# GpSimd writes the padding of q and k, two more PSUM banks, and a new order of steps in a fused attention and soft mixture-of-experts kernel

## The chip, the cores and the metric

The kernel runs on one core of one Trainium2 chip. The core has five engines that each work through a queue of their own: TensorE (PE, matrix products), VectorE (DVE), ScalarE (ACT), GpSimd (POOL) and SyncE (SP, which here only issues DMA transfers). Transfers go between the chip's memory and the on-chip buffers by sixteen DMA engines. The metric is the time of one execution on the device in microseconds (us), as the median of several runs. All times inside an execution are counted from the start of its span, the time from its first to its last instruction.

## The reference

Two stages, cut to what is computed:

```python
# attention over columns: B, N, C = 4, 5056, 256
qn = q / (norm(q, axis=1) + 1e-6)          # each column over all N rows
kn = k / (norm(k, axis=1) + 1e-6)
a = softmax(kn.T @ qn / tau)               # C x C for each batch
x = (v @ a).reshape(B * N, C)
# soft mixture of experts: 8 experts with 4 slots each, F = 1024
logits = x @ phi                           # (B*N) x 32
d = softmax(logits, axis=0)                # over all rows
slots = (d.T @ x).reshape(8, 4, C)
slot_out[e] = relu(slots[e] @ w1[e]) @ w2[e]
out = softmax(logits, axis=1) @ slot_out   # 20224 x 256
```

Every output row depends on the experts' output, and that on the softmax over all rows, so all of q, k and v must be read before the first output can be stored.

## The kernel before

Each batch is cut into ten units of 512 rows (UB = 10, UT = 512), so 5120 rows of which 5056 are real. The host pads q and k with zeros: in a batch's last unit (`u % 10 == 9`) the fourth of its four tiles of 128 rows has 64 real rows (HD = 64), and zeros in the other half. `load_qk` (L113) fetches a unit's q and k side by side in one transfer of 1 MB into one of five `raw` buffers (NRAW = 5). ACT casts and squares the unit (`cast` L177, `square` L208), DVE makes the low halves of a split into two reduced-precision parts and adds up the squares (`low` L183, `add` L214), PE adds k^T q into S (`score` L234). After ten units the batch's `att_` steps make the matrix a; GpSimd takes the root of the norms (L256).

v comes in both layouts, `v` (L126) and transposed `vt` (L132, L134); a part of the transposed tiles is turned on chip instead (`vTp` L359, `x` L364). PE makes the logits (L386), ACT copies them into `lg` (L405), DVE takes their running maximum (L415), ACT the exponentials (L449), DVE turns them into weights (L464), and PE gathers the slot sums (G, L486). A short run of `finish_`, `join_` and `last_` steps ends with the slots' inputs, `slT` (L604).

Then the experts. `up` (L672) makes H for the experts 0 to 3 (r = 0) and 4 to 7 (r = 1), each in two halves x of 512 columns: H0_0, H0_1, H1_0, H1_1. `relu` (L682) writes them to hs, `flip_h` (L688) turns hs into hTp, `back_h` (L694) copies that to hT, on DVE for x = 0 and on ACT for x = 1. `down` (L703) multiplies with w2 into O0 and O1, the two halves of the 256 output columns; each is 64 rows of the order, 128 instructions on PE. `o_copy` (L715) copies O to `ob` on DVE, `o_fold` (L719) spreads it on PE, and `o_back` (L725) writes `so` on ACT.

Beside this each batch has its softmax over the slots, on a tile `nat` of 128 x 1280: the transpose of the logits (L421), maximum, subtraction, exponential, sum, 1e-9 and reciprocal, product (`cm`, `cs`; L610 to L628), and the transpose back into `lg` (`c_flip`, L634). `out_mul` (L743) multiplies these with `so`, `out_evict` copies the result from PSUM into a tile `o` (ACT L765 for even g, DVE L767 for odd g), and `store` writes it. Batch 0's five tiles go in two half stores each of 512 KB, one for each half hf of the columns (L775), so that they may start when O0 is there and O1 is not; all others are stored whole, 1 MB each (L773).

PSUM has eight banks: S0, S1, T0, T1, LB, GB, X0, X1. O0 lies in T0 and O1 in T1. `out_mul` takes four banks for each product, in turn from the list `rings[hf]`, from place 4k on, where k counts the products.

All steps are entered in a list `plan` by `at(...)` and `tail(...)`. The table ORDER, 985 numbers, then says in which order they are called, and thus the order in each engine's queue. The first number given to `tail` has no part in it. All transfers are issued from SP's queue, in that order, and one that waits holds those behind it.

The lines that set the banks, the order and the two halves of the output:

```python
rings = {0: [S0, S1, LB, GB, T0, X0], 1: [S0, S1, LB, GB, T0, X0, T1, X1]}
t = bank(ring[(4 * k + g) % len(ring)], f"op{b}_{p}_{hf}_{g}")
for x in ORDER:
    key, _, f, a = plan[x]
    f(*a)
```

Of the kernel before, what the change touches and what calls it, by code (L numbers as in the profile page):

```python
# [17 lines left out]
UB = 10  # L18
# [11 lines left out]


ORDER = [
# [43 lines left out]
]  # L76


@with_exitstack
def colnorm_attention_soft_moe(  # L80
    ctx: ExitStack,
    tc: tile.TileContext,
    qk: bass.AP,
    v8: bass.AP,
    vt8: bass.AP,
    vt7: bass.AP,
# [26 lines left out]
    def load_qk(u, parts=((0, 4),)):  # L113
        b, i = divmod(u, UB)
        raw = apool.tile([P, 4, 2, C], F32, tag="raw", name=f"raw{u}", bufs=NRAW)
        for lo, hi in parts:
            src = qk[b, i][:, : 8 * C].rearrange("p (j x c) -> p j x c", x=2, c=C)
            sp.dma_start(raw[:, lo:hi], src[:, lo:hi])
        raws[u] = raw

    vs, vts = {}, {}
# [604 lines left out]


    OT = ["raw"] * 3 + ["hl"] * 3 + ["v"] * 6 + ["raw"] * 5 + ["hl"] * 3
    rings = {0: [S0, S1, LB, GB, T0, X0], 1: [S0, S1, LB, GB, T0, X0, T1, X1]}
    rings[None] = rings[1]  # L730
    ots, ops = {}, {}

# [277 lines left out]
        tail(28.07 + x, back_h, 1, x)  # L1010
        for r in range(2):
            for f in range(0, NF, 2):
                tail(30 + 5 * x + 2 * r + 0.1 * f, down, r, x, f)
        tail(34.6 + 5 * x, o_copy, x)
        tail(34.7 + 5 * x, o_fold, x)
        tail(34.8 + 5 * x, o_back, x)
# [76 lines left out]
```

## Time and profile before

| | |
|---|---|
| median of 3 runs | 284.16 us (283.67 to 284.9) |
| profiled execution | 283.62 us |
| its span | 281.8 us |
| mean granted TensorE clock | 0.951 |
| busy: PE, DVE, ACT, POOL | 251.1, 236.2, 189.8, 18.0 us |
| DMA | 114.55 MB in all, mean 406 GB/s |

How to read it: busy times are sums over an engine's instructions within the span. The profiled execution is one run more, with the profiler on; its span leaves out 1.8 us that lie around the first and last instruction. The share of the DMA is the mean over sixteen engines of the time that their packets took, which overlap a little, so that a full stretch reads 1.01 or 1.02.

### The profile page before, as it was taken

To read this page: it belongs to the slowest core of one execution; us is meant where nothing else is said; L and a number is where in the kernel's file an instruction comes from. 1 tells how busy PE (TensorE), PEld (TensorE's weight loads), DVE (VectorE), ACT (ScalarE), POOL (GpSimd) and SP (SyncE) were. 2 spreads that over 40 slices of the span, in tenths; PEclk is the share of its full clock that TensorE was granted. 3 is DMA by queue.
4 is the path that set the end of the run, shared out by engine and by line. 5 is a ranking of instruction groups with operands and counts; after the bars stand their busy time and mean duration, and the time that the engine had idled before them with its cause. 6 is when DMAs were issued, how large, how long until landed. Compare 5 with 4: busy or idle time off the path is not lost.

```text
span 281.8 us, 6011 instructions
## 1 busy us (share of the span) xinstructions
PE 251.1 (89%) x2446; PEld 204.7 (73%) x2446; DVE 236.2 (84%) x347; ACT 189.8 (67%) x273; POOL 18.0 (6%) x10
## 2 busy tenths in 40 slices
PE   8898999999999999999999999998989899659700
PEld 7687999999989989788686778755544778337500
DVE  1599999999999899999979695479988899998800
ACT  4879788889998978799687945647416237544600
POOL 0000000270003500020000001000000000000000
PEclk9999999999999999999999999999999999865955
DMA  7999999999999999999999999999999999999996
GB/s 279 428 414 417 422 422 413 421 416 420 419 417 421 416 420 417 420 420 409 408 411 419 414 419 412 417 416 416 419 412 408 406 363 359 417 419 417 416 420 259
DMA packets 19612, 114.55 MB, mean 406 GB/s; under 512 B 2305, under 2 KB 2305, under 8 KB 8961
## 3 DMA queue, kind: packets, MB, share of 16 engines
q1 hardware_dynamic: 19584, 114.17, 98.8%
q8 instruction: 19, 0.31, 0.4%
q14 instruction: 9, 0.07, 0.1%
HBM read 93.19 MB, written 20.97 MB: 405 GB/s over the span
## 4 chain that ended last, share of the span: by engine, by line
DVE 40%; PE 24%; issue 11%; ACT 9%; DMA 8%; POOL 2%; DVEq 0%; SPq 0%; ACTq 0%; POOLq 0%
DVE sq L214 15%; DVE hl L183 8%; DMA raw<-in_qk_dram 6%; PE S L234 5%; PE op_None L743 5%; ACT sq L208 3%; PE H L672 3%; PE O L703 3%; PE op L743 2%; POOL rn L256 2%; DMA vt<-in_vt_dram 2%; ACT hl L177 2%; DVE mxs L415 2%; DVE o L767 2%; ACT o L765 2%
## 5 line engine op out<-in xcount | busy, mean ns | idle before, releaser
L214 DVE TENSOR_TENSOR sq<-sq,sq 128x1024 f32<-128x1024 f32 (+1 forms) x63 | 84.6, 1371 | 3.0 <-ACT sq L208 2.6
L208 ACT ACTIVATE sq<-raw 128x2048 f32<-128x2048 f32 x40 | 75.9, 1909 | 12.0 <-DVE sq L214 8.1
L234 PE MATMUL S<-raw 128*128 128x256 f32 x312 | 75.1, 381 | 2.5 <-DMA raw<-in_qk_dram 2.5
L234 PE MATMUL S<-hl 128*128 128x256 f32 x468 | 68.4, 295 | 0.0
L234 PEld LDWEIGHTS S<-raw 128*128 128x128 f32 x312 | 56.1, 190 | 9.8 <-DMA raw<-in_qk_dram 3.8
L234 PEld LDWEIGHTS S<-hl 128*128 128x128 f32 x468 | 60.4, 190 | 3.0 <-issue 1.6
L183 DVE TENSOR_TENSOR hl<-raw,hl 128x1024 fp32r<-128x1024 f32 x39 | 46.8, 1217 | 7.9 <-ACT hl L177 7.9
L177 ACT CAST hl<-raw 128x1024 fp32r<-128x1024 f32 x39 | 40.1, 1040 | 7.0 <-PE S L234 4.1
L743 PE MATMUL op_None<-so,lg 32*128 32x256 f32 x240 | 24.2, 483 | 6.3 <-ACT o L765 2.4
L256 POOL TENSOR_TENSOR rn<-rn,half 128x4 f32<-128x4 f32 x4 | 17.3, 4313 | 154.4 <-DVE rn L251 154.4
L743 PEld LDWEIGHTS op_None<-so,lg 32*128 32x128 f32 x240 | 17.7, 230 | 12.0 <-ACT o L765 7.4
L765 ACT COPY o<-op_None 128x512 f32<-128x512 f32 x30 | 16.0, 591 | 11.6 <-PE op_None L743 10.1
L767 DVE COPY o<-op_None 128x512 f32<-128x512 f32 x30 | 18.8, 680 | 2.2 <-PE op_None L743 2.2
L486 PE MATMUL G<-v,dn 128*32 128x256 f32 x320 | 19.3, 381 | 0.0
L359 PE MATMUL vTp<-ident,v 128*128 128x128 f32 x112 | 16.9, 277 | 1.0 <-ACT x L364 0.8
L364 ACT COPY vt<-vTp 128x512 f32<-128x512 f32 x22 | 12.8, 581 | 7.2 <-PE vTp L359 7.2
L386 PE MATMUL L<-vt,M 128*32 128x256 f32 (+1 forms) x272 | 17.2, 380 | 0.1
L359 PEld LDWEIGHTS vTp<-ident,v 128*128 128x128 f32 x112 | 12.9, 141 | 4.6 <-issue 1.6
L486 PEld LDWEIGHTS G<-v,dn 128*32 128x32 f32 x320 | 10.0, 110 | 6.5 <-issue 0.7
L386 PEld LDWEIGHTS L<-vt,M 128*32 128x32 f32 x272 | 8.3, 109 | 6.6 <-issue 1.3
L405 ACT COPY lg<-L 128x256 f32<-128x256 f32 x20 | 7.0, 371 | 6.7 <-PE L L386 5.5
L765 ACT COPY o<-op 128x256 f32<-128x256 f32 x20 | 6.4, 379 | 7.0 <-PE op L743 7.0
(115 smaller groups left out, 248.8 us busy)
## 6 DMA issues: line engine op xcount, KB each, us to landing
raw<-in_qk_dram SPq DMA_DIRECT2D x40, 1024.0 KB, 9.2
v<-in_v_dram SPq DMA_DIRECT2D x20, 1024.0 KB, 10.8
out_dram<-o SPq DMA_DIRECT2D x15, 1024.0 KB, 8.7
vt<-in_vt_dram SPq DMA_DIRECT2D x19, 512.0 KB, 9.1
w<-in_moe_w_dram SPq DMA_DIRECT2D x16, 512.0 KB, 11.3
w<-in_moe_w_dram SPq DMA_DIRECT2D x8, 1024.0 KB, 15.6
out_dram<-o SPq DMA_DIRECT2D x10, 512.0 KB, 4.4
vt<-in_vt_dram SPq DMA_DIRECT2D x4, 480.0 KB, 11.4
```

Source lines behind the costliest of these rows:

```text
L177: act.copy(hl[:, :ns, 0::2, :], raws[u][:, :ns])
L183: dve.tensor_tensor(hl[:, :ns, 1::2, :], raws[u][:, :ns], hl[:, :ns, 0::2, :].bitcast(F32), op=ALU.subtract)
L208: act.activation(sq, raws[u], AF.Square)
L214: dve.tensor_tensor(a[:, lo:hi], a[:, lo:hi], s[:, lo:hi], op=ALU.add)
L234: pe.matmul(sm, w, x, start=first, stop=False, skip_group_check=True)
L256: pool.tensor_tensor(rn, rn, half, op=ALU.pow)
L359: pe.transpose(tp[:, P * jj : P * jj + P], vs[p][:, 4 * h + jj, P * m : P * m + P], ident)
L386: pe.matmul(L[S * g : S * g + S, :n, :], M[:, m, :], x[:, :n, S * g : S * g + S], start=m == 0, stop=m == 1,)
L486: pe.matmul(gp[S * g : S * g + S, :C], dn[:, x, j, :], vt[:, j, :], start=x == 0 and j < G, stop=x == n - 1 and j >= G,)
L743: pe.matmul(ops[b, p, hf, g][:, h, :], cT[b][S * g : S * g + S, 4 * i : 4 * i + 4, :].rearrange("s j t -> s (j t)"), so[S * g : S * g + S] ...
L765: act.copy(dst, src)
L767: dve.tensor_copy(dst, src)
```

## The change

Three edits. `load_qk` no longer fetches the zeros of each batch's last unit: GpSimd fills rows 64 to 127 of the fourth tile, one transfer (128 x 1536 elements, 768 KB) brings the first three tiles, and another (64 x 512, 128 KB) the real half of the fourth. The bank list of the first half's products has twenty places, the four of each product k = 0 to 4 in turn: product 2 takes T1 and X1 besides T0 and X0, of which T1 is O1's, so O1 must wait until that product is copied out. The third edit is a new table ORDER. All line numbers from L119 on move by 4 or 5 in the changed kernel.

```diff
@@ ORDER
-    626, 1, 0, 7, 2, 4, 3, 13, 23, 5, 8, 12, 11, 14, 22, 41, 32, 9, 10, 18, 19, 756, 16, 17, 34, 35, 20, 21, 25, 26,
+    626, 1, 0, 7, 2, 4, 13, 5, 14, 8, 9, 10, 22, 3, 11, 12, 18, 19, 32, 23, 590, 587, 16, 17, 21, 31, 25, 26, 29, 30,
...
@@ load_qk
         raw = apool.tile([P, 4, 2, C], F32, tag="raw", name=f"raw{u}", bufs=NRAW)
+        src = qk[b, i][:, : 8 * C].rearrange("p (j x c) -> p j x c", x=2, c=C)
+        if i == UB - 1:
+            parts = ((0, 3),)
+            pool.memset(raw[HD:, 3], 0.0)
         for lo, hi in parts:
-            src = qk[b, i][:, : 8 * C].rearrange("p (j x c) -> p j x c", x=2, c=C)
             sp.dma_start(raw[:, lo:hi], src[:, lo:hi])
+        if i == UB - 1:
+            sp.dma_start(raw[:HD, 3], src[:HD, 3])
...
-    rings = {0: [S0, S1, LB, GB, T0, X0], 1: [S0, S1, LB, GB, T0, X0, T1, X1]}
+    rings = {0: [S0, S1, LB, GB, T0, X0, S0, S1, T0, X0, T1, X1, LB, GB, T0, X0, S0, S1, LB, GB], 1: [S0, S1, LB, GB, T0, X0, T1, X1]}
...
-                tail(30 + 5 * x + 2 * r + 0.1 * f, down, r, x, f)
+                tail(30 + 6 * x + 2 * r + 0.1 * f, down, r, x, f)
```

What the table moves is read from each engine's queue. On PE, first, at the end of the products H. The rows before, the last four of H1_1 and what follows (names are tile, experts, half; w1_4 is expert 4's first matrix):

```order
L672 MATMUL H1_1_2237<-w1_4_2152,slT_116 32x512
L672 MATMUL H1_1_2237<-w1_5_2222,slT_116 32x512
L672 MATMUL H1_1_2237<-w1_6_2220,slT_116 32x512
L672 MATMUL H1_1_2237<-w1_7_2224,slT_116 32x512
L688 MATMUL hTp0_0_2250<-ident_88,hs0_2189 128x128 x4
L688 MATMUL hTp0_1_2269<-ident_88,hs0_2189 128x128 x4
L688 MATMUL hTp1_0_2281<-ident_88,hs1_2226 128x128 x4
L688 MATMUL hTp1_1_2293<-ident_88,hs1_2226 128x128 x4
L703 MATMUL O0_2305<-w2_0_2259,hT0_2255 32x128
```

And after the change, from the last row of H1_0 on:

```order
L676 MATMUL H1_0_2236<-w1_7_2224,slT_116 32x512
L692 MATMUL hTp0_1_2245<-ident_88,hs0_2199 128x128 x4
L692 MATMUL hTp0_0_2251<-ident_88,hs0_2199 128x128 x4
L676 MATMUL H1_1_2258<-w1_4_2129,slT_116 32x512
L676 MATMUL H1_1_2258<-w1_5_2220,slT_116 32x512
L676 MATMUL H1_1_2258<-w1_6_2233,slT_116 32x512
L676 MATMUL H1_1_2258<-w1_7_2224,slT_116 32x512
```

The turning of the first experts' h now stands ahead of H1_1, which follows in eight rows. Behind these come 16 of O0's 64 rows, then hTp1_0 and hTp1_1, and then O0's other 48 rows.

ACT's queue in the same place, before (hs is the relu, nat the exponential of one batch's softmax, its number the batch):

```order
L682 ACTIVATE hs0_2189<-H0_0_2208,rz_114 128x512
L616 ACTIVATE nat2_2204<-nat2_2204 128x1280
L682 ACTIVATE hs1_2226<-H1_0_2227,rz_114 128x512
L682 ACTIVATE hs1_2226<-H1_1_2237,rz_114 128x512
L694 COPY hT0_2255<-hTp0_1_2269 128x512
L616 ACTIVATE nat3_2087<-nat3_2087 128x1280
L694 COPY hT1_2286<-hTp1_1_2293 128x512
```

And after:

```order
L686 ACTIVATE hs1_2235<-H1_0_2236,rz_114 128x512
L698 COPY hT0_2256<-hTp0_1_2245 128x512
L620 ACTIVATE nat2_2222<-nat2_2222 128x1280
L686 ACTIVATE hs1_2235<-H1_1_2258,rz_114 128x512
L698 COPY hT1_2310<-hTp1_1_2305 128x512
L620 ACTIVATE nat3_2226<-nat3_2226 128x1280
```

The copy hT0 has moved ahead of both exponentials, batch 2's exponential stands behind the relu of H1_0 and ahead of that of H1_1, and batch 3's behind the copy hT1. On DVE, in the same stretch, the transpose (L421) of batch 3's logits has moved from ahead of slT to behind it, next to that of batch 2; the order there is two transposes, two maxima, the subtraction of batch 2, hT0, the subtraction of batch 3, the sum of batch 2, hT1, reciprocal and product of batch 2, ob; and three small steps for rz (L586 to L588) now stand ahead of slT.

DVE's queue from the copy ob of the first half on, before (o_4 is batch 0's fifth tile, op its product with first or second half of the columns and g; `lg_111` is batch 3's tile and `lg_110` batch 2's):

```order
L715 COPY ob_2370<-O_2305 128x128
L628 TENSOR_TENSOR nat_2204<-nat_2204,cs_2277 128x1280
L767 COPY o_4_2388<-op_4_0_1_2377 128x256
L767 COPY o_4_2388<-op_4_0_3_2379 128x256
L767 COPY o_2_2407<-op_2_0_1_2396 128x256
L767 COPY o_2_2407<-op_2_0_3_2398 128x256
L767 COPY o_0_2425<-op_0_0_1_2414 128x256
L767 COPY o_0_2425<-op_0_0_3_2416 128x256
L628 TENSOR_TENSOR nat_2087<-nat_2087,cs_2289 128x1280
L634 STREAM_TRANSPOSE lg_111<-nat_2087 128x768
L634 STREAM_TRANSPOSE lg_111<-nat_2087 128x512
L767 COPY o_1_2446<-op_1_0_3_2437 128x256
```

And after:

```order
L719 COPY ob_2366<-O_2274 128x128
L624 TENSOR_REDUCE cs_2369<-nat_2226 128x40
L771 COPY o_4_2395<-op_4_0_1_2384 128x256
L771 COPY o_4_2395<-op_4_0_3_2386 128x256
L628 TENSOR_SCALAR cs_2369<-cs_2369 128x40
L629 RECIPROCAL cs_2369<-cs_2369 128x40
L771 COPY o_2_2415<-op_2_0_1_2404 128x256
L632 TENSOR_TENSOR nat_2226<-nat_2226,cs_2369 128x1280
L771 COPY o_0_2432<-op_0_0_1_2419 128x256
L771 COPY o_0_2432<-op_0_0_3_2421 128x256
L638 STREAM_TRANSPOSE lg_110<-nat_2222 128x768
L771 COPY o_1_2484<-op_1_0_3_2475 128x256
```

Batch 3's sum and product are now spread among the first copies, and its transposes come later. Behind the last row come the other copy of o_1, a transpose of 768 columns, the second copy of o_2, the second ob, and the two copies of o_3. SP issues the half stores in the order o_4, o_0, o_1, o_2, o_3, and then the second halves of o_2 and o_1; before it was o_4, o_2, o_0, o_1, o_3. On PE the products of the first half are now p = 4, 2, 0, then half of O1's rows, product 1, the other half, product 3; before they were 4, 2, 0, 1, all of O1, 3. Among the loads, the last ones of v and vt (v15, x18) are issued with one load of w1 less ahead of them; the order of the first three w2 loads of 512 KB, which come early, has also changed.

## Rows read from the trace of the kernel before

**Rows 1.** From the page: the head, the main DMA queue of part 3 (packets, MB, share of 16 engines), the line on memory below it, and of part 6 the q/k loads (count, KB each, median us from issue to landing).

```profile
span 281.8 us, 6011 instructions
...
q1 hardware_dynamic: 19584, 114.17, 98.8%
...
HBM read 93.19 MB, written 20.97 MB: 405 GB/s over the span
...
raw<-in_qk_dram SPq DMA_DIRECT2D x40, 1024.0 KB, 9.2
```

**Rows 2.** The table of stretches: from and to in us, length, then busy us (and instructions) of PE, PE's weight loads, DVE, ACT and POOL, the granted TensorE clock, the DMA share and GB/s.

```profile
0.00:5.00 5.00, 3.95 (x18) 3.92 (x18) 0.98 (x7) 1.49 (x2) 0.70 (x6) 1.00 0.63 218
30.00:180.00 150.00, 149.49 (x1232) 129.40 (x1234) 137.59 (x183) 121.89 (x151) 17.25 (x4) 1.00 1.02 417
190.00:198.00 8.00, 6.59 (x96) 4.15 (x88) 7.82 (x17) 6.31 (x17) 0.00 (x0) 1.00 1.01 415
222.00:229.00 7.00, 5.70 (x132) 4.77 (x132) 5.95 (x10) 2.85 (x9) 0.00 (x0) 1.00 1.02 406
229.00:235.00 6.00, 5.18 (x152) 4.48 (x146) 5.54 (x14) 2.18 (x8) 0.00 (x0) 1.00 0.75 298
235.00:281.80 46.80, 24.92 (x270) 18.66 (x266) 29.80 (x45) 18.87 (x37) 0.00 (x0) 0.71 0.96 393
240.00:268.00 28.00, 20.07 (x193) 14.46 (x189) 25.02 (x36) 14.71 (x28) 0.00 (x0) 0.76 1.01 417
```

**Rows 3.** SP's own timeline: start and duration in us, line, what is issued. The sixth of the last thirteen w2 loads, and the first six half stores.

```profile
207.17 0.33 SPq L661 DMA_DIRECT2D w<-in_moe_w_dram  x1
...
224.91 0.35 SPq L775 DMA_DIRECT2D out_dram<-o  x1
225.97 0.34 SPq L775 DMA_DIRECT2D out_dram<-o  x1
227.05 0.33 SPq L775 DMA_DIRECT2D out_dram<-o  x1
230.69 0.33 SPq L775 DMA_DIRECT2D out_dram<-o  x1
232.59 0.33 SPq L775 DMA_DIRECT2D out_dram<-o  x1
234.17 0.33 SPq L775 DMA_DIRECT2D out_dram<-o  x1
```

**Rows 4.** DVE's timeline from slT on: start and duration in us, line, operation, out and in, count, and in brackets the idle time before it and what ended that.

```profile
207.56 0.19 DVE L604 COPY slT<-slp 128x32 f32<-128x32 f32 x1 [0.86 <-PE slp L595]
208.19 1.50 DVE L421 STREAM_TRANSPOSE nat<-lg 128x1280 f32<-128x1280 f32 x1
209.73 1.49 DVE L610 TENSOR_REDUCE cm<-nat 128x40 f32<-128x1280 f32 x1
211.25 1.49 DVE L613 TENSOR_TENSOR nat<-nat,cm 128x1280 f32<-128x1280 f32 x1
...
216.45 0.69 DVE L694 COPY hT<-hTp 128x512 f32<-128x512 f32 x1 [0.79 <-PE hTp L688]
217.06 1.48 DVE L620 TENSOR_REDUCE cs<-nat 128x40 f32<-128x1280 f32 x1
218.57 0.18 DVE L624 TENSOR_SCALAR cs<-cs 128x40 f32<-128x40 f32 x1
218.79 0.40 DVE L625 RECIPROCAL cs<-cs 128x40 f32<-128x40 f32 x1
219.11 0.63 DVE L694 COPY hT<-hTp 128x512 f32<-128x512 f32 x1
...
222.12 0.29 DVE L715 COPY ob<-O 128x128 f32<-128x128 f32 x1 [0.34 <-PE O L703]
222.32 1.48 DVE L628 TENSOR_TENSOR nat<-nat,cs 128x1280 f32<-128x1280 f32 x1
224.09 0.76 DVE L767 COPY o<-op 128x256 f32<-128x256 f32 x2 [0.29 <-PE op L743]
...
232.42 0.97 DVE L634 STREAM_TRANSPOSE lg<-nat 128x768 f32<-128x768 f32 x1
```

**Rows 5.** POOL's timeline: the fill of a 128 x 128 tile, and the root of the first batch's norms.

```profile
0.73 0.20 POOL masks.py:197 MEMSET ident<- 128x128 f32 x1 [0.29 <-POOLq L1050]
...
54.33 7.61 POOL L256 TENSOR_TENSOR rn<-rn,half 128x4 f32<-128x4 f32 x1 [53.03 <-DVE rn L251]
```

**Rows 6.** PE's timeline: the logits of a tile that is turned on chip, and the experts' products.

```profile
197.73 0.64 PE L386 MATMUL L<-x,M 128*32 128x256 f32 x8 [0.62 <-ACT x L364]
...
207.93 7.84 PE L672 MATMUL H<-w,slT 128*32 128x512 f32 x64
215.70 1.16 PE L688 MATMUL hTp<-ident,hs 128*128 128x128 f32 x8
217.28 1.13 PE L688 MATMUL hTp<-ident,hs 128*128 128x128 f32 x8 [0.43 <-DVE hT L694]
218.35 3.70 PE L703 MATMUL O<-w,hT 128*32 128x128 f32 x128
```

**Rows 7.** The view of one source line, L661 between 207.0 and 207.5 us, which holds the one load of rows 3: us from its issue to its landing.

```profile
DMA to landing us min/median/max: 12.6/12.6/12.6
```

**Rows 8.** ACT's timeline: the exponential of one batch's softmax.

```profile
212.77 1.27 ACT L616 ACTIVATE nat<-nat 128x1280 f32<-128x1280 f32 x1 [0.45 <-DVE nat L613]
```

83 rows, old and new, of the table ORDER are left out of this document.

## The prediction

> **What bounds the kernel now.** I read the page's head and its table of queues first [rows 1]: one queue carries 114.17 MB and its packets fill 98.8% of sixteen engines' span, so the end moves only if bytes go away or if the queue's idle time does. The table of stretches [rows 2] says where that idle time is: the first 5 us (218 GB/s), the stretch 229 to 235 us (share 0.75, 298 GB/s), and the last landing. Elsewhere the share is 1.02 or so: full. From 30 to 180 us PE is busy for 149.49 of 150 us as well, so PE and the queue are both near their limit there; loads run ahead of their users, with 9.2 us from issue to landing of a q/k load at the median [rows 1].
>
> The hole at 229 to 235 us lies where loads end and stores begin. From 235 us to the end 46.8 us at 393 GB/s are 18.39 MB, all of it output; of the 20.97 MB written, 2.58 MB thus moved earlier, 1.79 MB of them in 229 to 235 (6 x 298), and the other 0.79 MB took 1.95 us at 406 GB/s, so the data of the loads ended near 227.1 us. A half store (512 KB, 0.524 MB) takes 1.29 us at 406 GB/s. The first three were issued at 224.91, 225.97 and 227.05 [rows 3], behind loads, and ran 227.1 to 231.0; the fourth was issued only at 230.69, the fifth at 232.59, the sixth at 234.17. With 0.75 us from issue to first data (an estimate, chosen so that about five stores are through by 235, as the bytes say) they ran 231.45 to 232.75, 233.35 to 234.65, 234.9 to 236.2, and the seventh ended at 237.5. From there the queue stays full: DVE has 25.0 of 28 us to do in 240 to 268, and from 268 us or before nothing computes while the stores run on to 281. So the number to be forecast is when the seventh half store is through.
>
> What sets the store issues is a chain through the moment T at which the first half of the experts' output is copied (ob, L715; 222.12 before), 2.79 us ahead of the first store [rows 3, 4].
>
> **The change part by part.** *Bytes.* Four loads lose 128 KiB each, 0.524 MB: 1.26 us at the 417 GB/s of 30 to 180 us. The loads' data would end at 227.1 - 1.26 = 225.85. By itself that is worth nothing: the first three stores would be through at 229.7 and the fourth still begins 0.75 us after 230.69.
>
> A load into 64 partitions alone isn't in the trace. Its 128 KiB cost 0.31 us at the rate of the full ones; at half that rate they cost 0.63, which is what leaving them out saves, and the saving is gone. I take the first, for want of a row that shows less than the full rate in any long stretch, and keep both ends. [...]
>
> *The zero rows.* A fill of 64 x 512 elements on GpSimd, four times. The fill of 128 x 128 took 0.20 us at the start [rows 5]; four times the columns make 0.8 us, an estimate. Upper bound: the 128 x 4 instruction that took 7.61 us at 54.33 beside a busy DVE. Either is hidden by the 9.2 us from issue to landing of the load, since the fill waits for the same free buffer; uncovered, it would hold the square and the matmuls of that unit by the difference. On GpSimd's queue it stands ahead of each batch's root of the norms (L256), whose inputs come after that unit anyway. Four more issues on SP cost 0.33 us each of a queue that mostly waits. I take nothing.
>
> *The order ahead of slT (207.56).* PE's instructions ahead of the experts' first product are the same in number and shape, so PE can gain only idle time: 1.41 us of 190 to 198 [rows 2], of which 0.62 was a wait for a turned tile [rows 6]. The last v/x loads now go ahead of one 1 MB load of w1, and land some 1 to 4 us earlier. DVE loses a 1.50 us transpose from this stretch and takes three small instructions. Bounds for slT: 0 to 1.4 us earlier; I take 0.4, on the side of the wait of 0.62, so slT at 207.16.
>
> *From slT to T.* Three chains must be through. PE: from 207.93 to 222.05 are 14.12 us, 0.43 of them a wait for a copy [rows 6]; the new order puts the third product between, takes that wait away and adds none. So T = 207.16 + 0.37 (slT to PE's start) + 13.69 + 0.07 = 221.3. DVE [rows 4]: two transposes, two maxima and a subtraction (2 x 1.50, 2 x 1.49, 1.49: 7.47), hT 0.69, the second subtraction 1.49, one sum 1.48, hT 0.63, 0.18 + 0.40, one product 1.48: 13.8, so T = 221.1. The weights: the second half of the products of O0 needs the sixth w2 load, which landed at 207.17 + 12.6 = 219.8 [rows 3, 7]; with 1.26 us of bytes less ahead of it 218.5, and half of 3.70 us after that T = 220.4. The latest counts: T = 221.3, against 222.12.
>
> *From T to the stores.* The first one 2.79 us behind T, as before: issue 224.1. Behind it DVE's queue is new. Up to the second store: ob 0.29, sum 1.47, two copies 0.76, 0.18 + 0.40, one copy 0.38, product 1.48, two copies 0.76, with gaps 5.9: issue 227.2. Then a transpose of 768 columns 0.97 and two copies: 228.95; transpose and one copy: 230.3; the next at 231.3, 232.8 and 233.55. The two more banks let the product for the second tile run without waiting for copies, and the second half O1 is now cut in two parts of 1.85 us with a product between: PE's wait goes, and DVE's copies are what is late next. Data: 225.85 to 227.15; 228.0 to 229.3; 229.7 to 231.0; 231.05 to 232.35; then without a hole 233.65, 234.95, 236.25. Against 237.5 that is 1.25 us earlier. The later stores are the same bytes, behind a full queue: 283.62 - 1.25 = 282.4 for a profiled execution. The median of the runs was 284.16, 0.54 above the profiled one, so the forecast is 284.16 - 1.25 = **282.9**. Between T = 220.4 and T = 224 the gain is about 222.55 - T: each us of T counts in full, since the third and fourth store wait for their copies and not for the queue.
>
> **The rivals.** *The hole closes further.* If PE makes use of all its idle time (slT 1.3 us earlier or more), the weights set T = 220.4: gain 2.15, 282.0; if they too land sooner, the seven stores run on from 225.85 without a hole to 234.9: gain 2.6, 281.6. For it: the last v/x loads land earlier, and 1.41 us of PE's time stood idle there. Against: PE's work ahead is the same to the instruction, and it was busy for all but half a us of 150.
>
> *Slower: the new order makes T late.* The place is ACT's queue, where an exponential of 1.27 us [rows 8] stands ahead of the relu of H1_1 (of H1_0's too, before). Its input, DVE's subtraction, comes behind a second transpose and a second maximum now, near 214.8 by the sums above, so that it ends at 216.1; H1_1 is through at 216.5. So there are 0.4 us to spare, 0.6 with the 16 rows of O0 that PE has meanwhile. Behind the relu wait the turning of h, both copies hT and the rest of O0: each us by which DVE is later than 0.6 goes into T. It is slower than before from T = 222.55 (DVE 1.9 us late), by over 0.5% from T = 224.0 (285.6). For it: DVE has no idle time left between slT and T, and two transposes stand in front now. Against: all of its inputs there are early, and DVE waited 0.79 us for PE in this stretch before.
>
> *The saving in bytes isn't one* (half-height loads at half rate). Then the loads' data end at 227.1 and the sixth w2 load lands at 219.8: T = 219.8 + 1.85 = 221.65, gain 0.9, 283.3. It also caps the first rival there. [...]
>
> *No change at all:* the hole merely moves, because copies and O1 meet on DVE and PE (T as before, 222.1, gives 0.4 us, 283.7).
>
> **How the numbers follow.** About 0.5% (1.4 us) is what a measurement of this kernel can tell from no change; the forecast lies 1.25 us down, just inside. Forecast case 0.43, with a range of its own of 282.3 to 283.3 (slT 0.6 us to either side less what the weights cap); closing hole 0.28; saving lost 0.10; no change 0.07; slower 0.12. Faster by over 0.5% needs T below 221.1: the closing hole and a third of the forecast case, 0.43; within 0.5%: 0.44; slower: 0.13. The range leaves out a tenth on either side: from a little below 281.6, to 285.0 (T = 223.4).
>
> **What would show it.** In the profile after: loads with 98% share up to 226 us; slT near 207.2, the copy ob near 221.3, the first store near 224.1, the second near 227.2, the fourth near 230.3; between 227 and 231 us a smaller hole of some 1.3 us in total where 229 to 235 was; compute over by 267 us, long before the last store. T right and the time wrong would refute the account of the stores; a fill on GpSimd that squares or matmuls wait for would refute the cover; a load of 64 partitions with twice the time for its bytes would show the third rival. The forecast is wrong at once if the queue runs dry anywhere between 30 and 220 us.

## The result

The changed kernel takes 286.4 us (median of 8 runs, 285.57 to 287.16), the kernel before 284.13 us on the same chip (8 runs, 283.25 to 284.9): ratio 1.0084, 95% interval 1.0062 to 1.0107. It is slower by 0.8%, and outside the forecast range, which ends at 285.0. The profiled execution took 285.9 us, its span is 284.1. Head, queue and memory lines of its page, which answer to [rows 1]:

```profile
span 284.1 us, 6053 instructions
...
q1 hardware_dynamic: 19904, 113.65, 98.7%
...
HBM read 92.67 MB, written 20.97 MB: 400 GB/s over the span
```

The 0.52 MB are gone, and yet the queue is as full as before (98.7%): it moved less at 400 GB/s instead of 405. So the packets took longer. The table of stretches of the changed kernel, cut around its four small loads and at the end (columns as in rows 2):

```profile
20.00:35.00 15.00, 14.63 (x89) 13.05 (x88) 14.16 (x9) 11.74 (x9) 0.00 (x0) 1.00 1.02 397
45.00:60.00 15.00, 13.91 (x91) 12.88 (x90) 14.73 (x17) 11.39 (x9) 2.39 (x2) 1.00 1.02 398
83.00:98.00 15.00, 15.00 (x124) 13.40 (x123) 14.97 (x18) 12.75 (x12) 2.35 (x2) 1.00 1.01 392
125.00:140.00 15.00, 14.93 (x145) 11.31 (x144) 13.46 (x21) 13.17 (x17) 2.44 (x2) 1.00 1.02 391
...
222.00:229.00 7.00, 6.24 (x178) 5.33 (x166) 6.20 (x11) 2.82 (x8) 0.00 (x0) 1.00 0.99 393
229.00:235.00 6.00, 4.91 (x129) 3.96 (x126) 4.72 (x11) 1.49 (x6) 0.00 (x0) 1.00 0.87 350
...
264.00:269.00 5.00, 4.92 (x44) 3.75 (x36) 3.12 (x6) 2.09 (x4) 0.00 (x0) 0.54 0.92 377
```

The same cuts of the kernel before:

```profile
20.00:35.00 15.00, 14.17 (x90) 12.87 (x89) 14.90 (x9) 13.18 (x10) 0.00 (x0) 1.00 1.01 419
45.00:60.00 15.00, 15.00 (x101) 14.08 (x100) 15.00 (x16) 12.65 (x9) 5.67 (x1) 1.00 1.02 420
83.00:98.00 15.00, 15.00 (x111) 13.65 (x104) 14.02 (x19) 13.75 (x12) 6.40 (x1) 1.00 1.02 419
125.00:140.00 15.00, 14.91 (x149) 11.39 (x148) 14.83 (x20) 12.77 (x17) 1.45 (x1) 1.00 1.01 410
...
264.00:269.00 5.00, 2.25 (x29) 1.78 (x26) 3.02 (x6) 2.42 (x6) 0.00 (x0) 0.90 1.02 421
```

Look at the share and the rate together. At each of the four loads the share is full, 1.01 or 1.02, while the rate falls: between 410 and 420 GB/s before, between 391 and 398 now. The engines are busy and slow, not idle. That is 0.7 to 1.0 us of each 15 us, 3.2 us in all (15 x (1 - rate / rate before), summed). The second thing is the stretch 264 to 269: full before, with a share of 0.92 now, and PE is busy for nearly all of it (4.92 of 5 us).

DVE's timeline at slT and at the copy ob; then PE's where something held it: a q/k load, a load of w1, the last load of w2, and late in the output a transpose of the softmax:

```profile
209.13 0.19 DVE L608 COPY slT<-slp 128x32 f32<-128x32 f32 x1
...
223.74 0.29 DVE L719 COPY ob<-O 128x128 f32<-128x128 f32 x1 [0.47 <-PE O L707]
```

```profile
57.39 0.92 PE L238 MATMUL S<-raw 128*128 128x256 f32 x3 [1.09 <-DMA raw<-in_qk_dram]
...
214.10 1.91 PE L676 MATMUL H<-w,slT 128*32 128x512 f32 x12 [0.15 <-DMA w<-in_moe_w_dram]
...
230.75 1.93 PE L707 MATMUL O<-w,hT 128*32 128x128 f32 x58 [0.62 <-DMA w<-in_moe_w_dram]
...
262.99 5.93 PE L747 MATMUL op_None<-so,lg 32*128 32x256 f32 x48 [4.37 <-DVE lg L638]
```

PE's weight loads (PEld) at that load of w1, in the changed kernel and then in the kernel before:

```profile
214.10 0.16 PEld L676 LDWEIGHTS H<-w,slT 128*32 128x32 f32 x8 [1.06 <-DMA w<-in_moe_w_dram]
```

```profile
212.14 0.22 PEld L672 LDWEIGHTS H<-w,slT 128*32 128x32 f32 x8 [0.63 <-DMA w<-in_moe_w_dram]
```

And SP's first four half stores, which answer to [rows 3]:

```profile
226.54 0.35 SPq L779 DMA_DIRECT2D out_dram<-o  x1
229.40 0.34 SPq L779 DMA_DIRECT2D out_dram<-o  x1
230.93 0.33 SPq L779 DMA_DIRECT2D out_dram<-o  x1
232.08 0.33 SPq L779 DMA_DIRECT2D out_dram<-o  x1
```

slT was forecast at 207.2 and came at 209.13, T at 221.3 and came at 223.74. The stores stand where the sum puts them behind T: 2.80, 5.66, 7.19 and 8.34 us, where 2.8, 5.9, 7.65 and 9.0 were said.

A ledger helps from here on. For every packet of the main queue I took what it needed above the usual time of its size (314 ns for 8 KB, 236 for 6 KB, 161.5 for 4 KB, 80 for 2 KB), summed from 10 us on, with what faster packets needed less taken off, and divided by sixteen engines: the time lost in slow packets. Beside it stands the time in which engines had nothing to do, 10 to 270 us.

| kernel | slow packets, us | idle, us | bytes left out, as us at 417 GB/s |
|---|---|---|---|
| before | 1.37 | 1.56 | 0 |
| changed | 4.54 | 2.21 | 1.26 |
| e1, new order, full loads | 1.83 | 3.14 | 0 |
| e2, old order, changed load | 5.24 | 2.40 | 1.26 |
| e4, new order, 112 partitions | 10.42 | 2.21 | 1.26 |
| e5, old order, two halves | 21.71 | 4.85 | 0 |
| e6, old order, every other partition | 1.90 | 12.42 | 1.26 |
| e16, old order, every other partition in two batches | 1.60 | 1.28 | 0.63 |
| e17, as e16 with the lower partitions | 2.45 | 1.77 | 0.63 |

Against before, the changed kernel loses 3.17 us in slow packets and 0.65 in holes and saves 1.26: 2.6 us, about the 2.3 by which it is longer. Most of the loss is not in the small loads themselves: their 2 KB packets took 104 ns in the mean (85 in e16 below), which is some 0.3 us of the 3.2; the rest lies in packets of 4 to 8 KB beside them.

### The profile page after: what moved, and what is told of

It reads as the page before. It is cut to its first block, busy times and chain, and to the rows that moved or that the text cites. A ratio compares the mean times of both kernels' runs of the same rounds, so it can differ in the third digit from the quotient of the medians.

```text
span 284.1 us, 6053 instructions
## 1 busy us (share of the span) xinstructions
PE 252.8 (89%) x2446; PEld 205.4 (72%) x2446; DVE 236.5 (83%) x347; ACT 189.8 (67%) x273; POOL 9.4 (3%) x14
## 3 DMA queue, kind: packets, MB, share of 16 engines
q1 hardware_dynamic: 19904, 113.65, 98.7%
## 4 chain that ended last, share of the span: by engine, by line
PE 37%; DMA 34%; DVE 14%; ACT 7%; issue 4%; DVEq 0%; SPq 0%; ACTq 0%
PE S L238 23%; DMA w<-in_moe_w_dram 14%; DMA raw<-in_qk_dram 11%; DMA vt<-in_vt_dram 9%; PE op_None L747 6%; DVE sq L218 5%; ACT sq L212 4%; DVE o L771 3%; DVE hl L187 2%; PE L L390 1%; ACT hl L181 1%; PE vTp L363 1%; PE op L747 1%; PE G L490 1%; ACT o L769 1%
## 5 line engine op out<-in xcount | busy, mean ns | idle before, releaser
L238 PE MATMUL S<-hl 128*128 128x256 f32 x468 | 70.9, 298 | 0.9 <-DVE hl L187 0.9
L238 PEld LDWEIGHTS S<-hl 128*128 128x128 f32 x468 | 61.1, 190 | 4.6 <-DVE hl L187 1.3
L490 PEld LDWEIGHTS G<-v,dn 128*32 128x32 f32 x320 | 10.6, 110 | 6.0 <-issue 0.5
L747 PE MATMUL op<-so,lg 32*128 32x128 f32 x160 | 8.0, 292 | 4.4 <-ACT o L769 3.4
L260 POOL TENSOR_TENSOR rn<-rn,half 128x4 f32<-128x4 f32 x4 | 6.6, 1654 | 146.4 <-DVE rn L255 146.4
```

The source lines that it names most:

```text
L238: pe.matmul(sm, w, x, start=first, stop=False, skip_group_check=True)
L490: pe.matmul(gp[S * g : S * g + S, :C], dn[:, x, j, :], vt[:, j, :], start=x == 0 and j < G, stop=x == n - 1 and j >= G,)
L747: pe.matmul(ops[b, p, hf, g][:, h, :], cT[b][S * g : S * g + S, 4 * i : 4 * i + 4, :].rearrange("s j t -> s (j t)"), so[S * g : S * g + S] ...
```

## The experiments

The first theory after the result: the transfer into 64 partitions alone (A) slows the packets around it. Its rivals: the new order makes the kernel late (B), or short runs or the cut in two do it (C).

**Parts of the change apart (e1, e2, e3).** e1 is the changed kernel with the load of before. e2 is the kernel before with the changed load. e3 is e1 with this load, both pieces at full height and no fill:

```diff
         if i == UB - 1:
-            parts = ((0, 3),)
-            pool.memset(raw[HD:, 3], 0.0)
+            parts = ((0, 3), (3, 4))
         for lo, hi in parts:
             sp.dma_start(raw[:, lo:hi], src[:, lo:hi])
-        if i == UB - 1:
-            sp.dma_start(raw[:HD, 3], src[:HD, 3])
```

Expected of e1: 

> The changed kernel with the loads of before: each last unit comes whole (1 MB, zeros included), no fill on GpSimd, no 64-partition transfer; order and banks are the new ones. Theory A (the transfer into 64 partitions alone slows the packets around it, by 0.84 us a batch by their summed excess in the trace after): the data of the loads end near 227, as before, no stretch before 220 us under 410 GB/s, the sixth w2 load lands near 219.8, the copy ob near 221.7, and the time is 283.3 (0.3% faster than before), or up to 284.1. Theory B (the new order itself makes the kernel late): 285.5 to 286.4, as the changed kernel, with slT still near 209.

Expected of e2: 

> The kernel before, with the changed load alone: fill on GpSimd, 768 KB, and 128 KB into 64 partitions, in the old order with the old banks. Theory A: four holes of slow packets as in the changed kernel, loads through 2 us later than before (last w2 load landing 230.7 instead of 228.7), so the first store late by up to that and the time 285.3 to 286.4. Theory B: 283.7 to 284.2, no change.

Expected of e3: 

> As e1_full_loads, but each last unit in two transfers, both into all 128 partitions: three tiles (6 KB runs) and one tile (2 KB runs, 256 KB, zeros included). Theory A (it is the half height): as e1_full_loads within 0.5 us. Rival C (it is the 2 KB runs, or the cut in two): slow packets around these loads as in the changed kernel, 285.5 or more.

Measured: e1 285.22 us, ratio 1.0046 (1.0033 to 1.006); e2 287.04, 1.0127 (1.0091 to 1.0164); e3 284.45, 1.0017 (0.9994 to 1.004). The stretches of e1, in the table's columns:

```profile
20.00:35.00 15.00, 15.00 (x91) 13.47 (x90) 14.27 (x9) 12.05 (x10) 0.00 (x0) 1.00 1.01 418
45.00:60.00 15.00, 14.05 (x91) 12.96 (x90) 14.83 (x19) 12.53 (x11) 1.93 (x1) 1.00 1.00 391
83.00:98.00 15.00, 15.00 (x122) 13.40 (x122) 14.67 (x18) 12.49 (x12) 1.85 (x1) 1.00 1.02 416
125.00:140.00 15.00, 14.87 (x145) 11.16 (x144) 13.52 (x21) 13.24 (x17) 1.95 (x1) 1.00 1.01 418
```

With full loads three of the four slow stretches are gone, and in the old order the changed load brings them (3.9 us of slow packets over before): A holds for the load. e2 is even 0.6 us above what A had said for it. C falls: two pieces at full height, in 6 KB and 2 KB runs, cost nothing that can be seen (e3 against e1). But B holds too, in part: e1 is slower than before without any small load, and its second stretch stays at 391 GB/s. How much the order costs is less sure: e3 has the same order and no small load either, and can't be told from before. PE's timeline of e1 there:

```profile
56.97 1.99 PE L233 MATMUL S<-raw 128*128 128x256 f32 x8 [0.95 <-DMA raw<-in_qk_dram]
```

In the new order PE needs this load, issued at 50.88 us, when it lands at 56.9, and waits; in the old one it is busy for 149.49 of 150 us from 30 us on [rows 2]. It doesn't get the time back: slT is at 208.40 in e1, 0.84 us behind before, and at 208.24 in e3.

**Other ways to leave rows out (e4, e5, e6).** Theory D took shape here: what counts is not how many bytes go or how short the runs are, but that a transfer doesn't cover all 128 partitions evenly. e4 lays the 448 real rows out as 112 partitions with four rows each, in one transfer (`sp.dma_start(raw[:112], src[:112])`, with casts, squares, sums and products over 112 partitions); e5 keeps every byte and loads two halves, and e6 spreads the 64 rows, both in the kernel before and for the last units alone:

```diff
-            sp.dma_start(raw[:, lo:hi], src[:, lo:hi])
+            sp.dma_start(raw[:HD], src[:HD])
+            sp.dma_start(raw[HD:], src[HD:])
```

```diff
-            sp.dma_start(raw[:, lo:hi], src[:, lo:hi])
+            pool.memset(raw[:, 3], 0.0)
+            sp.dma_start(raw[:, :3], src[:, :3])
+            half = lambda t: t.rearrange("(h e) j x c -> h e j x c", e=2)[:, 0, 3]
+            sp.dma_start(half(raw), half(src))
```

Expected of e4: 

> The changed kernel, with the zeros left out in another way: the 448 real rows of a last unit are laid out as 112 partitions with four rows each, one transfer of 896 KB in 8 KB runs, and casts, squares, sums and products of that unit run over 112 partitions; no fill, no second transfer. The result is the same. Theory A in the form that only the half height costs: bytes saved at the full rate, loads' data end near 225.9, 282.9 or less. If any transfer that is uneven over the partitions costs: slow packets here as well, 284 to 286. Theory B: 285.5 or more.

Expected of e5: 

> The kernel before, but each batch's last unit is loaded by two transfers of 512 KB, into the first 64 partitions and into the other 64, in 8 KB runs, zeros included; no fill. Theory D (a transfer over fewer than 128 partitions gives its engines other partitions than a full one does, so that they meet the engines that are a load ahead or behind; by the run with 112 partitions, 2.2 us are lost for a load of 2.2 us): slow packets at all four places, 2 us or more a batch, 291 to 294. If the price is one for each such transfer (0.87 us, eight of them): 290 to 291. If 2 KB runs are needed for it: 284.2.

Expected of e6: 

> The kernel before, with the zeros left out, but the 64 real rows of the last half tile lie in every other partition: GpSimd fills all 128 rows of that tile, 768 KB for the three full tiles, then 128 KB in 2 KB runs into partitions 0, 2, 4 and so on, behind the fill. Theory D: each engine stays with its own partitions, no slow packets, loads through up to 1.2 us earlier than before, 283.5 to 284.2 (the hole behind the loads takes what is saved). If 64 descriptors, 2 KB runs or the fill do the harm: as with the changed load in the old order, 286 to 287.

Measured: e4 292.99 us, ratio 1.0324 (1.0302 to 1.0347); e5 306.26, 1.076 (1.0719 to 1.08); e6 293.3, 1.0324 (1.0293 to 1.0355). The first stretches of e4, then of e5:

```profile
20.00:35.00 15.00, 14.12 (x88) 12.64 (x87) 12.41 (x8) 10.34 (x9) 0.00 (x0) 1.00 1.02 371
45.00:65.00 20.00, 17.10 (x101) 15.60 (x100) 18.94 (x22) 14.57 (x12) 1.93 (x1) 0.92 1.00 363
```

```profile
20.00:35.00 15.00, 11.35 (x71) 10.07 (x69) 14.15 (x8) 9.78 (x7) 0.00 (x0) 1.00 1.02 327
45.00:65.00 20.00, 17.53 (x111) 16.01 (x110) 16.94 (x16) 13.12 (x10) 1.93 (x1) 1.00 1.02 315
```

Full share, low rate: e5 moves the same bytes as before and loses 20 us in slow packets; its time is far beyond every expectation written for it, and e4's far above the 284 to 286 said there for uneven transfers. e6 has lost as much time as e4, but by another cause. Its rate at the first two loads is 418 GB/s, without slow packets; nearly all of its loss is one hole, in this stretch, and POOL's timeline says why:

```profile
87.00:97.00 10.00, 9.16 (x62) 8.29 (x60) 9.03 (x13) 5.21 (x5) 6.87 (x2) 1.00 0.09 36
```

```profile
89.07 6.40 POOL L261 TENSOR_TENSOR rn<-rn,half 128x4 f32<-128x4 f32 x1 [27.08 <-DVE rn L256]
95.42 0.52 POOL L118 MEMSET raw<- 128x512 f32 x1
```

The fill stands behind the root of the batch ahead, which waits for DVE until 89.07 and takes 6.40 us. In e6 the transfer goes into the filled tile and must wait for the fill, and SP's whole queue waits with it. In the changed kernel fill and transfer touch different partitions, and its trace shows no such hole: the share is 1.01 at 83 to 98 us.

**The partitions alone (e16, e17).** Both leave rows out in the batches 0 and 1 only, where no root is in the way; they differ in nothing but `half`: every other partition in e16, `t[:HD, 3]` in e17.

Expected of e16: 

> The kernel before with the load of e14. No slow packets near 30 and 52 us. By the prediction's sum 0.6 us less of bytes changes nothing in the old order: 283.6 to 284.3. If bytes count in full: 283.2 to 283.6.

Expected of e17: 

> As e16 in everything (the fill of the whole tile, the same queue order, sizes and runs), except that the 64 real rows go into partitions 0 to 63 instead of every other one. Theory D (which partitions each engine fills): slow packets near 30 and 53 us, 0.8 us each in the sum of their excess, and 1 to 2 us over e16. If the choice of partitions is without effect: as e16 within 0.3 us.

Measured: e16 284.41 us, ratio 0.9993 (0.997 to 1.0016); e17 284.65, 1.0036 (1.001 to 1.0061). The stretches of e16, then of e17:

```profile
20.00:35.00 15.00, 13.94 (x87) 12.64 (x87) 14.90 (x9) 12.95 (x10) 0.50 (x1) 1.00 1.02 418
45.00:60.00 15.00, 15.00 (x101) 14.11 (x100) 15.00 (x16) 12.66 (x9) 6.20 (x2) 1.00 1.02 418
```

```profile
20.00:35.00 15.00, 14.16 (x90) 12.87 (x89) 14.90 (x9) 13.16 (x10) 0.53 (x1) 1.00 1.01 403
45.00:60.00 15.00, 15.00 (x101) 14.08 (x99) 15.00 (x16) 12.67 (x10) 6.14 (x2) 1.00 1.02 400
```

Same fill, same queue, same sizes: 418 against 403 and 400 GB/s, at both places. So it is the choice of partitions that makes the packets slow, as D said. In the time the difference is not shown: D had said 1 to 2 us, the medians are 0.24 us apart, and the two intervals overlap. The profiled spans, 281.3 and 282.1 us, are of one execution each.

**Order and banks (e7, e9, e10).** To part the new order, I kept its two ends apart: steps of the experts, of the softmax of the batches 1 to 3, of products and stores are "late", all others the head.

```diff
-    for x in ORDER:
+    for x in [x for x in HEAD if not late(x)] + [x for x in TAIL if late(x)]:
```

e7 takes the old head and the new tail and banks, e9 the new head with the old tail and banks, e10 only the new banks; all with full loads.

Expected of e7: 

> Full loads; the steps up to slT and all loads in the old order, everything behind slT (experts, softmax of the batches 1 to 3, products, stores) in the new order with the new banks. If the new order's head is what costs (slT at 208.4 instead of 207.6, slow packets at 50 to 60 us): slT near 207.4, ob near 221.8, 283.4 to 284.2. If its tail costs (more holes behind 225 us): 284.8 to 285.3, with 3 us of idle DMA behind 225.

Expected of e9: 

> Full loads; the steps up to slT and all loads in the new order, everything behind slT in the old order with the old banks. If the new head costs: slT near 208.3, ob near 222.9, 284.8 to 285.2 with 1.6 us of idle DMA behind 225. If the tail costs: 284.0 to 284.4.

Expected of e10: 

> The kernel before with the new list of banks alone: old order, full loads. If the banks by themselves bring what the new tail brought (0.5 to 0.8 us): 283.2 to 283.6. If it is the order of the tail, and the banks only make room for it: 283.8 to 284.4.

Measured: e7 283.33 us, ratio 0.9966 (0.9948 to 0.9984), the only kernel here that is faster than before by more than its interval; e9 285.6, 1.0063 (1.0033 to 1.0093); e10 283.74, 0.9988 (0.9965 to 1.001), no difference that can be told. So the new tail with its banks gains 0.3%, the new head loses 0.6%, and the banks alone bring nothing that shows. (The profiled executions of e9 and e10 were some 2 us above their medians, so their traces are not used.)

**Leaving the bytes out without harm (e11 to e15).** The load of e16, in three batches (all but batch 2) or two.

Expected of e11: 

> As e7_old_head_new_tail, with 128 KiB less in three of the four last units (batch 2's, where GpSimd is held by its root, is loaded whole): the 64 real rows of the last tile lie in every other partition, behind a fill of the whole tile. If bytes count once the chain to T is short: loads through 0.9 us earlier, no slow packets, 282.4 to 283.0. If the queue's hole takes them: 283.0 to 283.6. If the fill holds SP's queue somewhere: 284 or more, with idle DMA before 220 us.

Expected of e12: 

> The changed kernel (new order, new banks), with its load replaced by that of e11. Theory A and D: no slow packets at the four places of the changed kernel, and what is left is the loss of the new head: 284.3 to 285.2, 1.2 to 2 us under the changed kernel. If leaving the bytes out hurts in any form: 286 or more.

Expected of e13: 

> The kernel before with the load of e11 alone, old order and banks. By the sum of the prediction the bytes are worth nothing here, since the fourth store waits for its copy: 283.6 to 284.2, with loads through near 226.2 instead of 227.1 and a hole behind them that is longer by as much. If the bytes count in full: 282.9 to 283.2.

Expected of e14: 

> Old head, new tail, new banks, and 128 KiB left out in the batches 0 and 1 alone (64 real rows in every other partition behind a fill of the whole tile; the fill is not held by GpSimd's root there). If the fill of batch 3 was what held the queue in e11: no idle DMA before 220 us, loads through 0.6 us earlier than in e7, 282.6 to 283.3. If bytes left out are worth nothing: 283.3.

Expected of e15: 

> The changed kernel's order and banks with the load of e14. Near e12, which left out three pieces: 284.0 to 284.6, and 0.6 to 1.2 us under e1 (full loads, same order).

Measured: e11 285.11 us, ratio 1.0031 (1.0012 to 1.005); e12 284.0, 0.9996 (0.998 to 1.0012); e13 285.45, 1.0066 (1.0031 to 1.0101); e14 283.51, 0.9983 (0.9963 to 1.0004); e15 284.19, 1.0004 (0.9982 to 1.0025). In the old head the fill of batch 3 holds the queue, as this stretch of e13 shows:

```profile
126.00:129.00 3.00, 3.00 (x24) 2.90 (x23) 2.97 (x4) 3.00 (x3) 1.12 (x2) 1.00 0.54 169
```

e11 has the same hole, so both tell of the fill and not of the bytes; e13's own expectation, 283.6 to 284.2, had not seen it coming. e12 is the cleanest test of the change's own intent: with another choice of partitions, and in three batches of four, the changed kernel is 2.4 us faster than as it is, and equal to before. It was expected at 284.3 to 285.2, with the whole loss of the new head left in it; its slT is only 0.17 us behind before. Its DVE rows for slT and ob, and those of e14:

```profile
207.73 0.18 DVE L608 COPY slT<-slp 128x32 f32<-128x32 f32 x1
...
221.90 0.29 DVE L719 COPY ob<-O 128x128 f32<-128x128 f32 x1 [0.47 <-PE O L707]
```

```profile
207.43 0.19 DVE L654 COPY slT<-slp 128x32 f32<-128x32 f32 x1 [0.86 <-PE slp L645]
...
221.47 0.29 DVE L765 COPY ob<-O 128x128 f32<-128x128 f32 x1
```

Neither e14 against e7 nor e16 against before shows what 0.26 MB less are worth: all within their intervals. In the old order, worth nothing is what the sum had said.

## Why the prediction was wrong

**The load.** This is the step that failed first: "I take the first, for want of a row that shows less than the full rate", with the ends 0.31 and 0.63 us for a piece of 128 KB. The direction had a rival (the saving in bytes isn't one), but its price was bounded at zero. In fact the piece costs its neighbours too: 0.7 us of slow packets for each in the changed kernel (4.54 less the 1.83 that its order has with full loads, a quarter of it), 1.0 in the old order (e2: 5.24 less 1.37), 0.4 in e17 (2.45 less 1.60, a half), against the 0.31 that the bytes left out save. No run shows the half rate that stands behind the 0.63 us and the third rival; its sign, twice the time for the bytes, did not come: the small load's own packets took 104 ns in the mean, against 85 in e16. In the same order the change from full loads to the small ones costs 0.4% (1.0084 against e1's 1.0046; 0.7% against e3's 1.0017), and with other partitions that cost is gone (e12). The error was to bound the price of a transfer by its own length, as if the queue's other packets went on at their own pace.

Half rate doesn't give the size of the loss either. An estimate by it: e5, all of whose last units would go at half the rate, would lose 4 x 2.5 us (1 MB at 417 GB/s once more), and it lost 20 us in slow packets (21.71 less 1.37). Nor does the number of partitions alone: 112 of them lost 8.6 us more than e1 (10.42 less 1.83), and with 64 in both, e17 lost 2.45 us and e16 1.60. That engines meet in the same partitions, as theory D has it in the expectation of e5, was a conjecture, and no run shows it: the traces don't say which engine writes where, and the cause stays open beyond the choice of partitions.

**The order ahead of slT.** "I take 0.4" earlier: with full loads it came 0.84 us later (e1; 0.68 in e3), with the small ones 1.57, and 0.17 later in e12; in no run of the new order was it earlier. I had argued that PE's work is the same and so only its idle time can go; I had not asked where the new order would make new idle time. It does so at 57 us, 0.95 us in e1; and the waits that it was to take away at 190 to 198 us stayed, with PE busy for 6.59 of 8 us there in the changed kernel as before. Why packets are slow between 52 and 58 us there even with full loads stays open.

**From slT to T.** The order of the steps did what was forecast, but the time of H was read wrongly. slT to T takes 14.17 us in e12 and 14.04 in e14, where 14.13 was forecast. It takes 14.57 in e1, 14.61 in the changed kernel, and 15.05 to 15.38 in e3, e7, e11 and e15. What differs most is the first 48 products H: 5.55 us in e14, 6.12 in e12, 6.50 in e1 and 6.55 in the changed kernel. There PE's weight loads wait for a load of w1, 1.06 us in the changed kernel, 0.63 in e12 and not at all in e14. The same wait stood in the kernel before, 0.63 us of its 7.84 [rows 6]; e16, without it, needs 7.16 for the 64 products. The sum took 7.84 over as PE's work and named only the sixth w2 load among the weights. That one, issued at 209.11 and landed at 221.70, did not hold PE, which ran O0's last 96 instructions without a wait. In e7 and e11, two of the four kernels with over 15 us, the granted clock fell between slT and T: to 0.50 from 208 to 210 us in e7, as the last section shows, and to 0.88 in the mean of 208 to 222 us in e11, where e12 had 1.00.

**Behind T.** The first four stores were issued within 0.7 us of their forecast distance from T. The fifth and sixth came 10.5 and 12.1 us behind T, where 10.0 and 11.5 were said. "PE's wait goes, and DVE's copies are what is late next" failed there: the second part of O1 waits 0.62 us for the last w2 load, issued at 220.45 and landed at 230.71, and e12 has the same wait, 0.51 us. "From there the queue stays full" fell too, by some half us: in the new tail batch 1's softmax and products come last, its transpose starts at 261.86 (252.46 before), PE waits 4.37 us for it, and from 264 to 269 the share is 0.92 instead of 1.02. The last copy of an output ends at 274.4 us, where compute was to be over by 267. With 222.55 - T the changed kernel would have been 1.2 us slower than before; it was 2.3. The late fifth and sixth store and this hole, about half a us each, would make up the rest; that they add up is argued, not shown.

**The bytes.** That the saving is worth nothing by itself is consistent, in the old order, with e16 (0.9993, 0.997 to 1.0016), for half of them. **The fill** is hidden in the changed kernel, as said: 0.53 us where 0.8 was estimated. **The slower rival**, ACT's exponential ahead of the relu, was not what happened: between slT and T PE has no wait for ACT in the changed kernel's trace, and slT to T was as short as forecast in e12 and e14.

## What to carry to other kernels

Transfers into the lower 64 or 112 of the 128 partitions cost more here in slow packets (2.7 and 8.6 us over e1) than the bytes they left out could save (1.26 us): look at share and rate together, where a full share with a low rate (1.02 at 315 GB/s in e5) was slow packets and a low share (0.09 in e6's hole) a wait, and if rows are left out, try spreading the rest over the partitions. A duration read from a trace can hold a wait: look at the weight loads too before taking it over as an engine's work. That a saving of bytes counts only if the stretch that ends last waits for bytes is the sum's statement; no run here parts it from the noise. When a new order touches everything, cut it at a point where all work must meet (here slT) and time head and tail apart: one of them may hide the other's loss.

## What else the runs showed

GpSimd's fill took 0.52 or 0.53 us for 64 x 512 and for 128 x 512 elements alike, and 0.20 for 128 x 128 [rows 5]: the columns counted, the rows didn't. The root of 128 x 4, 7.61 [rows 5] and 6.40 us in the kernel before for the first two batches, took 1.86 and 1.83 us in the changed one (1.93 and 4.13 in e12). And TensorE's granted clock fell inside the critical stretch in e7's profiled execution: it was 0.82 in the mean of 206 to 208 us, where PE's short products ahead of slT run, and 0.50 in the next two, while PE was busy all the time (the columns as in rows 2):

```profile
206.00:208.00 2.00, 2.00 (x17) 1.94 (x17) 1.07 (x8) 0.00 (x0) 0.00 (x0) 0.82 1.02 414
208.00:210.00 2.00, 2.00 (x13) 0.58 (x16) 2.00 (x3) 0.18 (x1) 0.00 (x0) 0.50 0.99 406
210.00:212.00 2.00, 2.00 (x20) 0.53 (x16) 1.97 (x2) 0.69 (x1) 0.00 (x0) 0.83 1.00 403
```

The first 48 products H took 6.67 us there, where e14, at 1.00 from 206 to 212 us, took 5.55. e7 is faster than before in spite of it.
